# One row of the second MLP matrix in two unequal transfers, ahead of the last eleven rows

## The chip, the cores and the metric

The kernel runs on one core of a Trainium2 chip. The metric is the device time of one execution in microseconds. The core has five engines with instruction queues of their own: PE (TensorE), DVE (VectorE), ACT (ScalarE), POOL (GpSimd) and SP (SyncE, which here issues nearly all DMAs). The DMAs are carried out by 16 DMA engines.

## The reference

One decoding step for 8 sequences of one token of width 576. An attention over a cached window and an MLP work on the tokens, and a gate mixes them.

```python
g = sigmoid((x * gate_w).sum(-1, keepdims=True))
# attention: 32 query heads, 16 cached heads, the last W = 2048 positions, width 128
q = (x @ wq) -> heads
p = softmax(q k^T / sqrt(128));  a = (p v) @ wo
# MLP: 576 -> 4608 -> 576
h = gelu(layernorm(x2) @ w1 + b1);  b = h @ w2 + b2
out = g * a + (1 - g) * b
```

In the kernel both branches take the same `x` (`A_x`). The caches are 8 x 16 x 8192 x 128 values of 2 bytes each, of which the last 2048 positions are read; `w2` is 4608 x 576.

## The kernel before, in words

A planner (`_Plan`) takes operations with dependencies and costs, simulates the engines, and so fixes the order of each engine's queue; `emit` writes the queues and puts a semaphore wait ahead of an operation for every other engine or DMA that it depends on. Operations on one engine run in the order of the plan.

All bulk data goes through one chain of DMAs on SP, each issued after the one before (`after=last_dma[-1:]`): the query matrix, the first MLP matrix, then by a list named `stream` the 16 key items and 16 value items of 4 MB each, four parts of the output projection, the second bias (`bias`, L734, eight rows of 576 values), and at last the second MLP matrix (`m2_chunk`, L738 to L754). They fill four slots of a large buffer in turn; a DMA into a slot waits until its last reader is done.

The second MLP matrix stands in memory so that partition p holds its rows 36 p to 36 p + 35; a "row" below is one of these 36 rows in each of the 128 partitions, 576 values or 1152 bytes per partition. `M_CUTS` cuts the 36 rows into transfers: `[[12, 12], [8, 3, 1]]`, that is two transfers of twelve rows into one slot, then eight, three and one into the next. Each transfer has a semaphore of its own (`t0` to `t4`) and is followed by a group of matmuls on PE (`AccGroup`, written at L565): two matmuls of 288 columns a row, added up in one PSUM bank. The group waits for its transfer and runs after the group before it. After the first twelve rows four dummy matmuls (`keep_warm`, L717) keep PE going. When all groups are done, DVE and ACT copy one half each of the result (L779, L780) and SP and ACT send it out (L782).

Of the kernel before, what the change touches and what calls it, by code (L numbers as in the profile page):

```python
# [38 lines left out]
class _Plan:  # L39
# [10 lines left out]
    def add(self, eng, fn, deps=(), name=None, cost=0.1, after=(), prio=0):  # L50
        op = _Op(eng, fn, deps, name, cost, after=after, prio=prio)
        op.idx = len(self.all)
        self.all.append(op)
        return op

    def dma(self, eng, fn, semkey, nbytes, deps=(), name=None, after=(), prio=0):
        op = _Op(eng, fn, deps, name, self.DMA_ISSUE, after=after, is_dma=True, dma_sem=semkey, nbytes=nbytes, prio=prio)
        op.idx = len(self.all)
        self.all.append(op)
        return op  # L60
# [121 lines left out]
def build_kernel(nc, A_x, A_k_cache, A_v_cache, A_wq, A_wo, B_x, B_w1, B_b1, B_w2, B_b2, gate_w, out):  # L182
    B, Sq, D = A_x.shape
# [10 lines left out]
    ND = 4  # L194
# [15 lines left out]
    with ExitStack() as es:  # L210
# [77 lines left out]
        def aoffs(name):  # L288
            return R[name][0] // 2
# [4 lines left out]
        def view(name, parts=128):  # L294
            o, n, dt = R[name]
            a = arena[0:parts, o // 2: o // 2 + (n * (2 if dt == BF else 4)) // 2]
            if dt == F32:
                a = a.bitcast(F32)
            return a
# [46 lines left out]
        def slot(s):  # L346
            return RAW[:, s * DE:min((s + 1) * DE, ND * DE + SE)]
# [8 lines left out]
        def col(i, parts=128):  # L356
# [10 lines left out]
        OC = 64  # L367

        eng_sems = {e: es.enter_context(nc.semaphore("sem_" + e)) for e in ENGS}
        dma_keys = ["x", "b", "b2", "wq", "w1", "out"] + ["s%d" % i for i in range(ND + 1)] + ["t%d" % i for i in range(5)]  # L370
        dma_sems = {k: es.enter_context(nc.semaphore("dma_" + k)) for k in dma_keys}

        P = _Plan()
        add, dma = P.add, P.dma
# [7 lines left out]
                   deps=[o_idf], name="r8", cost=0.2)  # L382
# [30 lines left out]
        for s in range(2):  # L413
            o_xz.append(add("dve", (lambda s=s: lambda e: e.tensor_copy(xz[:, s, :].rearrange("p (k z) -> p k z", z=2)[:, :, s], x_sb[:, 512:576]))(),  # L414
                            deps=dx + [o_xz0], name="xz%d" % s, cost=0.12))
# [12 lines left out]
        for s in range(2):  # L428
            o_yz.append(add("dve", (lambda s=s: lambda e: e.tensor_copy(yz[:, s, :].rearrange("p (k z) -> p k z", z=2)[:, :, s], y_bf[:, 512:576]))(),
                            deps=[o_y, o_yz0], name="yz%d" % s, cost=0.12))  # L430
# [117 lines left out]
        o_hT = add("dve", lambda e: e.transpose(view("hT"), bass.AP(arena, offset=aoffs("hb"), ap=[[AST, 128], [1, FT], [FT, 32]])), deps=[o_hf], name="hT", cost=1.3)  # L548
# [25 lines left out]
        for vi in range(Hkv):  # L574
# [2 lines left out]
                stream.append(("W", vi // NVW))  # L577
            if vi + 3 < Hkv:
                stream.append(("K", vi + 3))
        M_CUTS = [[12, 12], [8, 3, 1]]  # L580
        stream += [("B", 0)] + [("M", i) for i in range(len(M_CUTS))]

        last_dma = [d_w1r]
        slot_free = [[o_qp], [], [], [o_hp], [o_qp, o_hp]]
# [12 lines left out]
        def take_slot():  # L597
            n = n_slot[0]
            n_slot[0] += 1
            return (1, 2, 0, 3)[n % ND]  # L600
# [111 lines left out]
        def keep_warm(name, n, after):  # L712
            def fn(e):
                mm = None
                for k in range(n):
                    args = (ps[:, k % 4, :], zeros_bf, maskR)
                    mm = e.matmul(*args, start=True, stop=True, skip_group_check=True) if k == 0 else held_matmul(nc, e, *args, start=True, stop=True, skip=True)  # L717
                return mm
            return add("pe", fn, deps=[exp_done[NG - 1], o_z, o_mR], name=name, cost=0.22 * n, after=after)
# [11 lines left out]
        o_m2 = []  # L731
# [6 lines left out]
        def m2_chunk(ci):  # L738
            s = take_slot()
            j = sum(sum(c) for c in M_CUTS[:ci])  # L740
            at = 0
            src = B_w2.rearrange("(p j) n -> p (j n)", j=FT)
            ops = []
            for n, jn in enumerate(M_CUTS[ci]):
                d = dma("sp", (lambda j=j, jn=jn, at=at: lambda e: e.dma_start(slot(s)[:, at * D:(at + jn) * D], src[:, j * D:(j + jn) * D]))(),
                        "t%d" % (sum(len(c) for c in M_CUTS[:ci]) + n), 128 * jn * D * 2, deps=slot_free[s] if n == 0 else [], name="d_w2_%d_%d" % (ci, n), after=last_dma[-1:])
                last_dma.append(d)
                mms = [(hT[:, j + k, 0:8], slot(s)[:, (at + k) * D:(at + k + 1) * D]) for k in range(jn)]
                ops.append(AccGroup("m2_%d_%d" % (ci, n), mms, [o_hT, d], cost=0.25 * jn, after=o_m2[-1:]).op)
                o_m2.append(ops[-1])  # L750
                if j == 0:
                    o_m2.append(keep_warm("warm1", 4, [ops[-1]]))
                j, at = j + jn, at + jn
            slot_free[s] = ops  # L754
# [15 lines left out]
        for kind, i in stream:  # L770
            {"K": k_item, "V": v_item, "W": wo_chunk, "M": m2_chunk, "B": bias}[kind](i)
# [37 lines left out]
def bass_gated_mix__sliding_block_cached__mixer_channel_mlp__decode_kernel(  # L809
    nc: bass.Bass,  # L810
    A_x: bass.AP,
    A_k_cache: bass.AP,
    A_v_cache: bass.AP,
    A_wq: bass.AP,
    A_wo: bass.AP,
    B_x: bass.AP,
    B_w1: bass.AP,
    B_b1: bass.AP,
    B_w2: bass.AP,
    B_b2: bass.AP,  # L820
    gate_w: bass.AP,
    out: bass.AP,
):
    build_kernel(nc, A_x, A_k_cache, A_v_cache, A_wq, A_wo, B_x, B_w1, B_b1, B_w2, B_b2, gate_w, out)
# [28 lines left out]
```

## Time and profile before

| | us |
|---|---|
| median of 3 runs | 366.87 (366.44 to 367.72) |
| profiled execution, its own time | 366.56 |
| its span, first to last instruction | 364.7 |
| PE busy | 242.6 |
| DVE busy | 217.3 |
| matmuls of L565 (in all 140) | 12.6 |
| issue of the five transfers of L745 | 328.01 to 334.89 |
| last copy of the result (DVE, L779) begins | 362.55 |

The span runs from the first to the last instruction that the profile records; the profiled execution's own time has some two microseconds more around it. The page gives busy time per engine, the busy share of the DMA engines in 40 slices, the chain of work that ended last, and groups of instructions by line. 154.31 MB are read from memory in the span, 423 GB/s.

### The profile page before, as it was taken

The page shows a single profiled execution, that of the slowest core. Times are in us where ns is not written, and L with a number is a line of the kernel's source. Part 1 is how long each engine was busy: PE and PEld are TensorE (multiplying, and loading weights), DVE is VectorE, ACT ScalarE, POOL GpSimd, SP SyncE. Part 2 cuts the span into 40 slices and gives each one's busy share as a digit, 9 for nine tenths or more (in the row PEclk, how much of TensorE's full clock was granted, in tenths as well). Part 3 has the DMA queues.
Part 4 walks back from the last instruction along what each step waited for, and adds up shares of the span by engine and source line. Part 5 has one row for each costly group of instructions (what it writes and reads, how often), then busy time and mean ns, then how long its engine had stood idle before and what let it go on. Part 6 is the DMA issues. An engine that isn't in the chain of part 4 may idle for free.

```text
span 364.7 us, 2619 instructions
## 1 busy us (share of the span) xinstructions
PE 242.6 (67%) x1329; PEld 57.0 (16%) x893; DVE 217.3 (60%) x160; ACT 39.9 (11%) x46; POOL 23.2 (6%) x66
## 2 busy tenths in 40 slices
PE   0346566599397956859197956868197948686675
PEld 0100000122011121202011121202011220102232
DVE  0722999666884757266774657276766668284220
ACT  1012100400400040000400040000400040002000
POOL 7210001000100100001000100001000100000000
PEclk9985599699979976969778976969798976989699
DMA  8999999999999999999999999999999999999995
GB/s 348 432 410 429 431 431 431 431 431 430 429 431 431 429 428 431 433 431 433 429 431 431 433 431 429 431 433 431 431 429 431 426 431 429 431 431 431 426 437 244
DMA packets 10675, 154.48 MB, mean 424 GB/s; under 512 B 764, under 2 KB 932, under 8 KB 1320
## 3 DMA queue, kind: packets, MB, share of 16 engines
q1 hardware_dynamic: 10608, 154.29, 99.0%
q8 instruction: 9, 0.15, 0.1%
q10 hardware_dynamic: 56, 0.03, 0.0%
q14 instruction: 2, 0.02, 0.0%
HBM read 154.31 MB, written 0.01 MB: 423 GB/s over the span
## 4 chain that ended last, share of the span: by engine, by line
DMA 58%; DVE 22%; PE 15%; issue 2%; ACT 1%; ACTq 0%; POOL 0%; DVEq 0%
DMA arena<-in_A_k_cache_dram 49%; DVE arena L649 18%; PE ps L175 9%; DMA arena<-in_B_w_dram 7%; PE ps L661 2%; DMA arena<-in_gate_w_dram 2%; PE ps L683 2%; PE ps L486 1%; DVE arena L548 1%; DVE arena L622 1%; ACT ps L631 1%; PE ps L565 0%; ACT arena L522 0%; DVE arena L543 0%; DVE arena L506 0%
## 5 line engine op out<-in xcount | busy, mean ns | idle before, releaser
L649 DVE STREAM_TRANSPOSE arena<-arena 128x2048 f32<-128x2048 f32 x64 | 144.5, 2291 | 60.0 <-DMA arena<-in_A_k_cache_dram 38.6
L175 PE MATMUL ps<-arena 128*128 128x512 bf16 (+2 forms) x453 | 136.3, 457 | 39.7 <-DVE arena L649 36.6
L683 PE MATMUL ps<-arena 128*32 128x512 bf16 x512 | 60.3, 390 | 3.1 <-DVE arena L637 2.0
L661 PE MATMUL ps<-arena 128*128 128x512 bf16 x114 | 50.5, 443 | 17.7 <-DVE arena L649 17.7
L626 ACT ACTIVATE arena<-ps,arena 128x2048 bf16<-128x2048 f32 x8 | 15.7, 1967 | 239.5 <-DVE arena L625 239.5
L661 PEld LDWEIGHTS ps<-arena 128*128 128x128 bf16 x128 | 13.9, 109 | 171.0 <-DVE arena L649 113.5
L683 PEld LDWEIGHTS ps<-arena 128*32 128x32 bf16 x512 | 25.1, 99 | 46.6 <-issue 20.4
L622 DVE TENSOR_REDUCE arena<-ps 128x1 f32<-128x2048 f32 x8 | 18.3, 2286 | 12.5 <-PE ps L175 12.4
L616 POOL COPY arena<-arena 32x128 bf16<-32x128 bf16 x32 | 9.2, 287 | 212.7 <-PE ps L175 202.9
L633 DVE STREAM_TRANSPOSE arena<-arena 128x2048 bf16<-128x2048 bf16 x8 | 18.3, 2291 | 6.4 <-ACT arena L626 6.4
L693 DVE SCALAR_TENSOR_TENSOR arena<-ps,arena 128x512 f32<-128x512 f32 x8 | 6.0, 752 | 20.2 <-PE ps L683 20.2
L565 PE MATMUL ps<-arena 128*8 128x288 bf16 (+1 forms) x140 | 12.6, 339 | 7.1 <-DVE arena L708 5.8
L702 PE MATMUL ps<-arena 128*128 128x256 f32 x16 | 5.6, 431 | 16.0 <-POOL arena L698 16.0
L635 PE MATMUL ps<-arena 128*128 128x1 f32 x16 | 4.5, 353 | 15.1 <-ACT ps L631 14.3
L631 ACT ACTIVATE ps<-arena 128x2048 f32<-128x2048 f32 x7 | 13.1, 1875 | 0.1
L698 POOL TENSOR_TENSOR arena<-arena 128x256 f32<-128x256 f32 x8 | 4.9, 612 | 109.4 <-DVE arena L625 61.7
L440 PE MATMUL ps<-arena 8*128 8x8 bf16 x8 | 0.6, 171 | 14.7 <-DVE arena L414 9.6
L696 DVE TENSOR_REDUCE arena<-arena 128x128 f32<-128x512 f32 x8 | 8.4, 1047 | 0.3
L565 PEld LDWEIGHTS ps<-arena 128*8 128x8 bf16 (+1 forms) x140 | 6.4, 97 | 13.5 <-DVE arena L708 7.0
L705 ACT ACTIVATE arena<-ps,arena 64x256 bf16<-64x256 f32 x8 | 3.7, 464 | 42.9 <-PE ps L702 42.8
L708 DVE STREAM_TRANSPOSE arena<-arena 128x256 bf16<-128x256 bf16 x4 | 2.5, 632 | 9.8 <-ACT arena L705 9.8
L543 DVE TENSOR_TENSOR arena<-arena 128x1152 f32<-128x1152 f32 x1 | 1.4, 1359 | 11.3 <-ACT arena L541 11.3
(86 smaller groups left out, 64.5 us busy)
## 6 DMA issues: line engine op xcount, KB each, us to landing
arena<-in_A_k_cache_dram SPq DMA_DIRECT2D x16, 4096.0 KB, 28.0
arena<-in_A_v_cache_dram SPq DMA_DIRECT2D x16, 4096.0 KB, 32.6
arena<-in_B_w_dram SPq DMA_DIRECT2D x1, 4608.0 KB, 23.4
arena<-in_A_wo_dram SPq DMA_DIRECT2D x4, 1152.0 KB, 34.1
arena<-in_A_wq_dram SPq DMA_DIRECT2D x1, 4096.0 KB, 12.9
arena<-in_B_w_dram SPq DMA_DIRECT2D x2, 1728.0 KB, 27.7
arena<-in_B_w_dram SPq DMA_DIRECT2D x1, 1152.0 KB, 27.1
arena<-in_B_w_dram SPq DMA_DIRECT2D x1, 576.0 KB, 24.3
```

What stands on the lines that cost most here:

```text
L175: return e.add_instruction(mybir.InstMatmult(name=nc.get_next_instruction_name(), engine=mybir.EngineType.PE, ins=[e.lower_ap(rhs), e.lowe ...
L565: ins = e.matmul(ps[32 * j:32 * j + 8, BK_ACC, 0:JN], lhsT, rhs[:, JN * j:JN * j + JN], start=False, stop=True, skip_group_check=True, til ...
L616: return e.tensor_copy(dst, src)
L622: mx = add("dve", lambda e: e.tensor_reduce(out=k(MX), in_=ps[:, 0:4, :].rearrange("p a n -> p (a n)"), axis=AXL.X, op=ALU.max), deps=[qk_ ...
L626: ex = add("act", lambda e: e.activation(out=Pm, in_=ps[:, 0:4, :].rearrange("p a n -> p (a n)"), func=ACTF.Exp, bias=k(NB), scale=SCALE, ...
L631: mask_done[g + 1] = add("act", lambda e: e.activation(out=ps[:, 0:4, :].rearrange("p a (n c) -> p (a n) c", c=4), in_=bass.AP(arena_f, of ...
L633: pt_done[g] = add("dve", lambda e: e.transpose(bass.AP(arena, offset=aoffs("PT") + 2048 * (g % 2), ap=[[AST, 128], [8, 64], [512, 4], [1, ...
L649: tr = add("dve", (lambda h=h, kb=kb: lambda e: e.transpose(bass.AP(arena_f, offset=foffs("KT") + kb * 2048, ap=[[AST // 2, 128], [1, 2048]]),
L661: mm = e.matmul(*args, start=False, stop=True, skip_group_check=True) if rc == 0 else held_matmul(nc, e, *args, stop=True, skip=True)
L683: mm = e.matmul(ps[c:c + 32, BK_OS[g % 2], :], PT[:, g % 2, 16 * c + 32 * t:16 * c + 32 * t + 32], slot(s)[:, (j % 2) * SE + 512 * t:(j % ...
L693: vmul = add("dve", lambda e: e.scalar_tensor_tensor(out=vmv, in0=ps[:, BK_OS[g % 2], :].rearrange("p (r d) -> p r d", r=4), scalar=rr[:, ...
L696: acc_ev[g] = add("dve", lambda e: e.tensor_reduce(out=EV[:, g % 2, :], in_=vm.rearrange("p (r d) -> p d r", r=4), axis=AXL.X, op=ALU.add) ...
```

## The change

The last twelve rows are cut `[1, 7, 3, 1]` in place of `[8, 3, 1]`. The first of these four, one row, is fetched by two transfers: partitions 0 to 113 with semaphore `t6`, then partitions 114 to 127 with semaphore `t5`. As the change's description has it, the first uses six DMA engines (19 partitions each) and the second fourteen (one partition each). The row's group of two matmuls waits for both. The other rows follow as before in whole transfers, with semaphores `t2` to `t4`. SP thus issues seven transfers of the second matrix and not five.

```diff
-        dma_keys = [...] + ["t%d" % i for i in range(5)]
+        dma_keys = [...] + ["t%d" % i for i in range(7)]
...
-        M_CUTS = [[12, 12], [8, 3, 1]]
+        NSK = 114
+        M_CUTS = [[12, 12], [1, 7, 3, 1]]
...
             for n, jn in enumerate(M_CUTS[ci]):
-                d = dma("sp", (lambda j=j, jn=jn, at=at: lambda e: e.dma_start(slot(s)[:, at * D:(at + jn) * D], src[:, j * D:(j + jn) * D]))(),
-                        "t%d" % (sum(len(c) for c in M_CUTS[:ci]) + n), 128 * jn * D * 2, deps=slot_free[s] if n == 0 else [], name="d_w2_%d_%d" % (ci, n), after=last_dma[-1:])
-                last_dma.append(d)
+                parts = ((0, NSK, 6), (NSK, 128, 5)) if (ci, n) == (1, 0) else ((0, 128, 2 * ci + n - (ci > 0)),)
+                ds = []
+                for p0, p1, key in parts:
+                    d = dma("sp", (lambda j=j, jn=jn, at=at, p0=p0, p1=p1: lambda e: e.dma_start(slot(s)[p0:p1, at * D:(at + jn) * D], src[p0:p1, j * D:(j + jn) * D]))(),
+                            "t%d" % key, (p1 - p0) * jn * D * 2, deps=slot_free[s] if n == 0 else [], name="d_w2_%d_%d_%d" % (ci, n, p0), after=last_dma[-1:])
+                    last_dma.append(d)
+                    ds.append(d)
                 mms = [(hT[:, j + k, 0:8], slot(s)[:, (at + k) * D:(at + k + 1) * D]) for k in range(jn)]
-                ops.append(AccGroup("m2_%d_%d" % (ci, n), mms, [o_hT, d], cost=0.25 * jn, after=o_m2[-1:]).op)
+                ops.append(AccGroup("m2_%d_%d" % (ci, n), mms, [o_hT] + ds, cost=0.25 * jn, after=o_m2[-1:]).op)
```

More of the change, by code (lines that the diff above doesn't have):

```diff
@@ L369, in build_kernel @@
         eng_sems = {e: es.enter_context(nc.semaphore("sem_" + e)) for e in ENGS}
-        dma_keys = ["x", "b", "b2", "wq", "w1", "out"] + ["s%d" % i for i in range(ND + 1)] + ["t%d" % i for i in range(5)]
+        dma_keys = ["x", "b", "b2", "wq", "w1", "out"] + ["s%d" % i for i in range(ND + 1)] + ["t%d" % i for i in range(7)]
         dma_sems = {k: es.enter_context(nc.semaphore("dma_" + k)) for k in dma_keys}
```

## The prediction

> **What bounds the kernel now.** I read the page first, then the chain of waits, the timeline of the end, the issues of line 745, and busy time by stage.
>
> ```profile
> span 364.7 us, 2619 instructions
> DMA  8999999999999999999999999999999999999995
> q1 hardware_dynamic: 10608, 154.29, 99.0%
> q8 instruction: 9, 0.15, 0.1%
> ```
>
> The DMA engines are full from the second slice to the last, so the kernel lasts as long as its bytes, and an edit at the end of the stream counts only through the moment at which the last bytes are used. The chain of waits from 355 us says which moment that is:
>
> ```profile
> 333.61 27.14 DMA arena<-in_B_w_dram
> 360.75 0.04 issue
> 360.79 1.74 PE ps L565 x24
> 362.53 0.02 issue
> 362.55 0.45 DVE arena L779
> ```
>
> The end hangs on the landing of the eight-row transfer at 360.75 us. Its 16 matmuls, the 6 of the three-row and the 2 of the one-row transfer run without a pause (24 in 1.72 us, so 72 ns each); the rest, 362.53 to 364.73, is eviction and output. The timeline of PE and of SP:
>
> ```profile
> 357.98 1.64 PE L565 MATMUL ps<-arena 128*8 128x288 bf16 x24
> 360.79 1.72 PE L565 MATMUL ps<-arena 128*8 128x288 bf16 x24 [1.17 <-DMA arena<-in_B_w_dram]
> ...
> 328.01 6.88 SPq L745 DMA_DIRECT2D arena<-in_B_w_dram  x5
> ```
>
> PE is idle for 1.17 us before 360.79, and SP has issued all five second-matrix transfers by 334.9, over 24 us before the last part lands. Busy time by stage of the last two microseconds (last two columns: mean busy share of the 16 DMA engines, GB/s):
>
> ```profile
> 360.60:361.00 0.40, 0.21 (x4) 0.18 (x6) 0.00 (x0) 0.00 (x0) 0.00 (x0) 1.00 0.60 242
> 361.00:361.40 0.40, 0.40 (x10) 0.27 (x8) 0.00 (x0) 0.00 (x0) 0.00 (x0) 1.00 0.47 182
> 361.40:361.70 0.30, 0.30 (x10) 0.18 (x4) 0.00 (x0) 0.00 (x0) 0.00 (x0) 1.00 0.46 161
> 361.70:362.00 0.30, 0.30 (x8) 0.12 (x6) 0.00 (x0) 0.00 (x0) 0.00 (x0) 1.00 0.07 23
> ```
>
> 0.47 x 16 is 7.5: half of the engines are out of work by 361 us, the other half run to 361.8. A transfer lands when its slowest engine is done, so moving bytes from the late half to the early half would bring the end forward. All depends on which half the six engines belong to.
>
> **Which engines are late, and why.** The trace has a record of every DMA packet (queue, start, duration, bytes) without the engine's number. On one engine a packet starts 3 to 4 ns before the last one's end, so the packets can be strung into 16 chains. The bias transfer has 8 rows; eight chains carry its 1152-byte packets (347.6 to 349.2 us). The gate transfer of 6 rows marks six chains at 4.75 to 4.93 us, and following these to the end (the order of the chains' lags stays the same but for the jumps told below) leads to six of those eight. The last packet of each engine starts at (us):
>
> ```
> six engines with gate rows   360.31 360.34 360.58 360.74 361.10 361.64
> two more with bias rows      360.09 361.55
> the other eight              360.53 360.54 361.63 361.68 361.76 361.77 361.79 361.85
> ```
>
> The reason for the two halves is the queue of instructions: nine 16 KB packets (q8, above) at 32, 90, 129, 174, 220, 267, 306, 344 and 362 us. Each of the first eight puts one chain 1.41 to 1.43 us behind, for the rest of the run, since its queue never runs empty; two 8 KB fetches (83 and 180 us) cost 0.84 and 0.52 us. The fetch at 344 us hit one of the six.
>
> **The change part by part.** Durations are pitches of packets in the same records: 1152 bytes 47 ns, 3456 bytes 132, 9216 bytes 344, a transfer's end mark 6. That is 36.8 ps a byte and 4.4 ns a packet, so 8064 bytes (seven rows) cost 301.
>
> *Rows moved.* Before, each engine carries 8 x 344 + 6 = 2756 ns of the eight-row transfer. After, all carry 8 x 301.4 + 6 = 2417 for seven rows. 114 rows on six engines are 19 each: 19 x 47 + 6 = 897; 14 on fourteen are one each: 47 + 6 = 53. So the six go to 3367 (+0.61 us), eight others to 2470 (-0.29), and the two left out to 2417 (-0.34). The small-packet pitch is bounded by 42 ns (bytes alone: +0.51 in all) and 60 ns, the slowest of the undisturbed 1152-byte packets at the start (+0.88); 47 is taken, as it was measured in this stage.
>
> *The end, with these shifts.* Of the six, the latest ends at 361.64 + 0.61 = 362.25; of the others the latest moves from 361.85 to 361.56. The last packet is thus 0.40 us later than before. Packets' starts and landings lie 0.3 us apart here (361.85 and 362.13, the last of the 16 updates). With that lag seven rows land at 361.11, three at 362.17, one at 362.55. PE does 14 matmuls from 361.15 to 362.15, six from 362.21 to 362.64, two to 362.78. The same sum for before gives 362.47 (the profile: 362.53), so the change costs **+0.31 us**: less than 0.40 because the first row's two matmuls leave the tail.
>
> *That first row.* Its two landings come at about 358.7 (12 rows of the late one of the six done at 357.4, then 0.95 us, then the lag), PE is busy with the twelve rows before until 359.62, so the added wait for a second semaphore ends in the 1.17 us gap. Queued behind it on PE is only the rest of the second matrix. Without that cover it costs its two matmuls, 0.14 us.
>
> *Two more issues on SP.* Line 745's issues take 328 to 434 ns: 0.87 us more, done by 335.8, past nothing but the output issue at 363.02. Free; the cover is 22 us.
>
> *Two more transfers.* In a queue that is never empty nothing of a transfer's fixed price shows: the one-row transfer's last landing follows that of the three rows by 0.32 us (361.81 and 362.13 in the updates), and its bytes need 8 x 47 = 0.38. So two more are counted at nothing beyond their end marks. [...]
>
> **The sum.** Span 364.73 + 0.31 = 365.04; the profiled execution took 366.56, so 1.83 lie around the span: 366.87. That execution is 0.31 below the median of the three runs (366.87), on which the forecast stands: 366.87 + 0.31 = **367.2 us**. 0.3% is 1.1 us, about what a measurement of this kernel can tell from no change, so that counts as no change.
>
> **Rivals.**
> *All six are early (0.21).* If the fetches fall on other engines in other executions, and none of the 16 KB ones on the six, the latest of the six is the one at 361.10 + 0.61 = 361.71, the others end at 361.56; the seven rows land at 360.57 and PE ends at 362.24 (by the others alone at 362.09): -0.23 to -0.38 us, 366.5 to 366.6. For it: a single fetch, the one at 344 us, is all that stands against it here. Against: eight fetches on 16 engines would by chance nearly always hit one of six.
> *A fetch in the tail (0.06).* The ninth 16 KB fetch starts at 362.02, after the last data packet. The change has an engine of the six work until 362.25. If the fetch comes on a loaded one of the six, it adds its 1.42 us to the 0.31: 368.6, slower. It decides from the point where the fetch starts before that engine's last packets. Against: one engine in 16, and PE's progress, which it follows, is itself 0.3 us later.
> *Fixed time that shows (0.03).* At the start, with an empty queue, the 512 KB transfer lands 3.6 us after its issue (the issues' list), 1.2 of them for its bytes (32 KB an engine at 36.8 ps). If each of the two added transfers drained the queue for the other 2.4 us, the time would be 366.87 + 4.8 + 0.31 = 372.0. [...] Against: no gap stands between any two of the last transfers.
> *No shift (0.04).* If the 114 rows went eight to an engine as in whole transfers, there would be no skew; only 47 + 12 ns more, 366.9. For: no transfer of the trace has more than 16 rows and a count that 16 does not divide. Against: the six-row transfer ends on six updates.
> *Forecast (0.66).* Its own range is 366.8 to 367.8: the packet bounds (+0.22 and +0.57), and the runs' scatter (366.44 to 367.72).
>
> The whole range goes from 366.3, under the gain, to 367.9; outside lie the fetch, the fixed time and the far ends of the scatter. Faster by over 0.3% would need 1.1 us, and even a perfect levelling of the 16 ends above (mean 361.12, last 361.85) is worth 0.73: 0.04, for scatter. Slower: 0.13 (0.09 of the two rivals, 0.04 scatter). Same: 0.83.
>
> **What the changed profile would show.** Two matmuls of line 565 near 359.6, then 14, 6 and 2 from about 361.15, with short waits for DMA between them; the DMA share near 0.38 (six of 16) or less after 361.6 where it was 0.46; the last landing at 362.5; more packets of 1152 bytes (128 more). SP shows seven issues ending by 336. The forecast is wrong if the late engine is not of the six (last landing below 362.0), if the bias and gate chains were misread, or if the second part's transfer opens a gap between packets.

## The result, and the profile after

The change makes the kernel slower: 367.89 us, median of 9 runs (367.60 to 369.17), against 366.66 us for the kernel before (9 runs, 366.37 to 367.72). The ratio is 1.0036 (95% interval 1.0021 to 1.0051), so about 1.2 us where 0.3 was forecast. The forecast time was 367.2. The profiled execution took 367.60 us with a span of 365.8, so again 1.8 lie around the span; against the profiled execution of before it is 1.04 us longer.

The page of after, the lines that answer to those of before:

```profile
span 365.8 us, 2640 instructions
DMA  8999999999999999999999999999999999999995
q1 hardware_dynamic: 10756, 154.29, 98.9%
q8 instruction: 8, 0.13, 0.1%
```

The bytes of queue q1 are the same, in 148 more packets, and in tenths the DMA row is digit for digit that of before. Nothing on this page shows what happened.

The chain of waits of after, from 334 us on (start, length, what):

```profile
334.36 27.43 DMA arena<-in_B_w_dram
361.79 0.04 issue
361.83 1.02 PE ps L565 x14
362.86 0.04 issue
362.89 0.68 PE ps L565 x8
363.57 0.02 issue
363.59 0.45 DVE arena L784
```

On this chain the end still hangs on the first big transfer of the tail, now seven rows, which lands at 361.79. Fourteen matmuls follow at 73 ns, then PE waits for the three rows and does the last eight. Of these the last two start at 363.26, just behind the landing of the last row at 363.22, so that landing sets the end as well. All matmuls are done at 363.57, where the prediction had 362.78 and before had 362.53.

The timeline of PE (the bracket gives the idle time ahead and what ended it), of the weight loads (PEld) of its last two matmuls, and of SP's issues:

```profile
358.49 1.76 PE L565 MATMUL ps<-arena 128*8 128x288 bf16 x26 [0.63 <-DMA arena<-in_B_w_dram]
361.83 1.72 PE L565 MATMUL ps<-arena 128*8 128x288 bf16 x22 [1.58 <-DMA arena<-in_B_w_dram]
...
363.26 0.09 PEld L565 LDWEIGHTS ps<-arena 128*8 128x8 bf16 x2
...
328.06 15.69 SPq L749 DMA_DIRECT2D arena<-in_B_w_dram  x7
```

The first row's two matmuls have left the tail: 26 and 22 in place of 24 and 24. But the group before the tail is late too: it begins at 358.49, after a wait of 0.63 us for a DMA, where before it began at 357.98 without one. The second twelve rows, which the change does not touch, landed half a microsecond late (358.45 against 357.94), while the first twelve rows were still on time (353.85 against 353.84). So the loss begins ahead of the tail.

Busy time by stage shows where. The columns are window, length, busy shares of PE, PEld, DVE, ACT and POOL, TensorE clock, mean share of the DMA engines, and GB/s. First before, then after:

```profile
357.00:358.00 1.00, 0.83 (x5) 0.02 (x4) 0.00 (x0) 0.00 (x0) 0.00 (x0) 1.00 0.98 415
358.00:359.00 1.00, 1.00 (x18) 0.74 (x20) 0.00 (x0) 0.00 (x0) 0.00 (x0) 1.00 1.00 423
359.00:360.00 1.00, 0.62 (x11) 0.23 (x6) 0.00 (x0) 0.00 (x0) 0.00 (x0) 1.00 0.97 402
```

```profile
357.00:358.00 1.00, 0.87 (x4) 0.00 (x0) 0.00 (x0) 0.00 (x0) 0.00 (x0) 1.00 0.87 258
358.00:359.00 1.00, 0.51 (x10) 0.38 (x12) 0.00 (x0) 0.00 (x0) 0.00 (x0) 1.00 1.07 331
359.00:360.00 1.00, 1.00 (x22) 0.70 (x16) 0.00 (x0) 0.00 (x0) 0.00 (x0) 1.00 0.98 397
...
361.40:361.70 0.30, 0.00 (x0) 0.00 (x0) 0.00 (x0) 0.00 (x0) 0.00 (x0) 1.00 0.74 284
361.70:362.00 0.30, 0.17 (x4) 0.14 (x6) 0.00 (x0) 0.00 (x0) 0.00 (x0) 1.00 0.60 215
362.00:362.40 0.40, 0.40 (x10) 0.30 (x8) 0.00 (x0) 0.00 (x0) 0.00 (x0) 1.00 0.13 46
```

In the two microseconds from 357 on, when the packets of the split row are moved, the DMA engines are as busy as ever (0.87 and 1.07, where a packet is counted whole in one window) but move 258 and 331 GB/s in place of 415 and 423. The engines are occupied and slow. The records of single packets say it without the windows' edges:

```
packets that start from 355 to 362.5 us, after   shortest ns longest ns  (before: all alike)
13824 bytes (second twelve rows)                    516        691         516
 8064 bytes (seven rows)                            305        491     9216 bytes: 347
 1152 bytes (split row, last row)                    51         82          51
rate by 0.4 us from 357.0: 339 310 299 294 328 361 417 GB/s   (before: 430 427 429 429 428 424 424)
```

The first longer packet starts at 356.3 us. From 357.25 to 359.25 every data packet that starts, of whatever size, is longer than its like before, by 1.06 to 1.6 times, and by 1.5 on average at the worst; no packet takes as long as a microsecond there, so all 16 engines are hit. From 359.5 on all data packets are within 7% of their old length. Called the *excess* below: the time of all packets above their undisturbed time, over 16 engines. Here it is 0.61 us an engine.

### The profile page after: what moved, and what is told of

Its sections match the earlier page's. It is cut to its first block, busy times and chain, and to the rows that moved or that the text cites. A ratio compares the mean times of both kernels' runs of the same rounds, so it can differ in the third digit from the quotient of the medians.

```text
span 365.8 us, 2640 instructions
## 1 busy us (share of the span) xinstructions
PE 247.7 (68%) x1347; PEld 57.6 (16%) x893; DVE 217.1 (59%) x160; ACT 39.9 (11%) x46; POOL 23.2 (6%) x66
## 4 chain that ended last, share of the span: by engine, by line
DMA 58%; DVE 24%; PE 14%; issue 1%; ACT 1%; ACTq 0%; POOL 0%; SPq 0%; DVEq 0%
DMA arena<-in_A_k_cache_dram 49%; DVE arena L650 20%; DMA arena<-in_B_w_dram 7%; PE ps L175 7%; PE ps L662 2%; DMA arena<-in_gate_w_dram 2%; PE ps L684 2%; PE ps L486 1%; DVE arena L548 1%; DVE arena L623 1%; ACT ps L632 1%; PE ps L565 0%; ACT arena L522 0%; DVE arena L543 0%; DVE arena L506 0%
## 5 line engine op out<-in xcount | busy, mean ns | idle before, releaser
L662 PE MATMUL ps<-arena 128*128 128x512 bf16 x128 | 57.5, 450 | 51.3 <-DVE arena L650 51.2
```

Source lines behind the costliest of these rows:

```text
L662: mm = e.matmul(*args, start=False, stop=True, skip_group_check=True) if rc == 0 else held_matmul(nc, e, *args, stop=True, skip=True)
```

## The experiments

After this comparison two theories stood: the cost is the uneven load of the six engines alone, as forecast (and only its size was off), or the split transfer slows the whole stream while it is moved. For the second it was open what makes it: the count of partitions, the reads, small packets, or the place where the packets are written. Excess and longest packets below are worked out from the packet records of one profiled execution each; times are medians, and ratios are against the kernel before on the same chip.

**The change without the split.** `whole_row` keeps the cut `[1, 7, 3, 1]` and fetches the first row in one transfer of 128 partitions:

```diff
-                parts = ((0, NSK, 6), (NSK, 128, 5)) if (ci, n) == (1, 0) else ...
+                parts = ((0, 128, 6),) if (ci, n) == (1, 0) else ...
```

> Cuts 1, 7, 3, 1 as in the changed kernel, but the first row in one transfer of 128 partitions. In the profile of the change all packets between 357.0 and 359.4 us are stretched, 8064-byte ones from 305 to as much as 491 ns. Theory A (the six engines write into partitions that other engines are serving, and this slows all of them): no stretch here, 8064-byte packets at 305 ns; 0.1 to 0.2 us under the kernel before, since the first row's two matmuls leave the tail (-0.14). Theory B (the cut into one and seven rows slows the packets): the stretch stays, 0.4 to 0.8 us above the kernel before. Theory C (only uneven load counts, the stretch comes with it): as A here.

366.73 us, ratio 0.9998 (0.9986 to 1.0011). Busy time by stage:

```profile
357.00:358.00 1.00, 0.84 (x5) 0.10 (x1) 0.00 (x0) 0.00 (x0) 0.00 (x0) 1.00 0.98 395
358.00:359.00 1.00, 0.88 (x15) 0.60 (x16) 0.00 (x0) 0.00 (x0) 0.00 (x0) 1.00 0.98 412
```

No dip, all 128 packets of 8064 bytes at 305 ns. The new cut by itself is worth nothing that these runs can tell; the cost is that of the split. The 0.14 us expected of it do not show: PE ends at 362.74, 0.35 behind the landing of the last row (362.39), and that landing does not come earlier for the new cut (362.13 in before).

**The split with even load.** `split_112_16` has `NSK = 112`: 112 partitions, then 16. In the traces of before and after, transfers of 6, 8, 14, 114 and 128 partitions land with 6, 8, 14, 6 and 16 updates, each the largest number up to 16 that divides the partitions; by that count both parts here go over all 16 engines.

> The changed kernel with the first row split 112 + 16 partitions: by the count that divides, both parts go over sixteen engines, seven and one partitions each, so the load is even as before, but most engines write a few partitions that belong to the share of another engine in whole transfers. Theory A: a smaller stretch, some 0.1 to 0.4 us above the whole row. Theory C: no stretch, within 0.05 us of the whole row (one more packet and end mark per engine).

367.48 us, ratio 1.0011 (0.9999 to 1.0023). By that count every engine has the same load here, and yet packets are stretched (8064 bytes up to 486 ns, excess 0.38) and the rate dips:

```profile
357.00:358.00 1.00, 0.84 (x5) 0.06 (x1) 0.00 (x0) 0.00 (x0) 0.00 (x0) 1.00 1.01 348
358.00:359.00 1.00, 0.38 (x9) 0.28 (x10) 0.00 (x0) 0.00 (x0) 0.00 (x0) 1.00 1.06 353
```

So the stretch is not a matter of load. Against the kernel before, its time is within the measurement of no change; the packets show the stretch, and the spans of its twelve runs (365.1 to 365.8) lie at or above those of `whole_row` (364.6 to 365.1).

**Extra transfers.** The other runs but the last take the kernel *before* and issue one extra transfer ahead of the eight rows, into columns of the slot that nothing reads, with a semaphore that only the final wait looks at. The outputs do not depend on it. The frame is the same in all, and only the destination, source and byte count differ (`pad_from_chip` also depends on its constant):

```diff
+            if ci == 1:
+                pad = dma("sp", lambda e: e.dma_start(DESTINATION, SOURCE), "t5", ...,
+                          deps=slot_free[s], name="d_pad", after=last_dma[-1:])
+                last_dma.append(pad)
+                pads.append(pad)
...
-        add("sp", lambda e: e.sem_inc(eng_sems["sp"], 1), deps=fin, name="final_wait", cost=0.05)
+        add("sp", lambda e: e.sem_inc(eng_sems["sp"], 1), deps=fin + pads, name="final_wait", cost=0.05)
```

`pad_six_own` was meant to load six engines without mixing their partitions, `pad_six_spread` is shaped as the change's first part (102 partitions, 17 to an engine):

```diff
+ slot(s)[0:48:8, 12 * D:28 * D]     # pad_six_own, 16 pieces of 1152 bytes in each of 6 partitions
+ slot(s)[0:102, 12 * D:13 * D]      # pad_six_spread, src[0:102, 24 * D:25 * D]
```

> The kernel before (cuts 8, 3, 1), with one extra transfer ahead of the eight rows that nothing reads: partitions 0, 8, 16, 24, 32 and 40, sixteen pieces of 1152 bytes each, so six engines get 16 packets more (16 x 47 + 6 = 0.76 us) and each is meant to write a partition of its own share. Theory A: no stretch; the late one of the six ends 0.76 later, 0.55 past the latest before, so about +0.45 to +0.55 us. Theory C: stretch as in the change, +0.9 to +1.2 us.

> The kernel before with one extra transfer ahead of the eight rows that nothing reads: 102 partitions of 1152 bytes, 17 to each of six engines (17 x 47 + 6 = 0.81 us), written over partitions 0 to 101, that is mostly outside the share of the engine that writes. Theory A: the stretch comes back, +1.0 to +1.4 us. Theory C: the same as the six in their own shares plus 0.05.

368.26 us, 1.0034 (1.0021 to 1.0047), excess 0.61; and 367.72 us, 1.0027 (1.0017 to 1.0038), excess 0.55. Both stretch the stream (9216 bytes up to 716 and 596 ns). `pad_six_own` did not do what it was meant for: six partitions in steps of eight do not leave the stream alone. Six in steps of four do, in `pad_six_home` further down (347 ns).

Then count, reads and the source's place. 120 partitions from either end; 102 partitions from a constant in on-chip memory (`ones_bf`, 1024 bytes each), so that large memory is not read; and 102 partitions from one row of large memory (`B_b2`):

```diff
+ slot(s)[0:120, 12 * D:13 * D]          # pad_120_low
+ slot(s)[8:128, 12 * D:13 * D]          # pad_120_high
+ slot(s)[0:102, 12 * D:12 * D + 512]    # pad_from_chip, source ones_bf[0:102, :]
+ slot(s)[0:102, 12 * D:13 * D]          # pad_one_row, source B_b2.partition_broadcast(102)
```

> The kernel before with an extra transfer ahead of the eight rows that nothing reads: partitions 0 to 119, 1152 bytes each; 120 goes over fifteen engines, eight partitions each, so every engine stays in the share that it has in a transfer of 128. Theory A (writing outside the own share slows everything): packets of the eight rows stay at 347 ns; +0.3 to +0.4 us for the eight packets. Theory D (many short reads from scattered rows of memory by fewer engines slow everything): little or no stretch, since fifteen of sixteen read as in a whole transfer. Theory E (any transfer that is not spread over sixteen engines slows what follows): stretch, +0.9 us or more.

> The same with partitions 8 to 127: fifteen engines, eight partitions each, each engine now in the share of the next one. Theory A: stretch, the eight-row packets well over 347 ns, +0.8 us or more. Theory D: as partitions 0 to 119. Theory E: stretch in both.

> The kernel before with an extra transfer of 102 partitions, 1024 bytes each, copied from a constant tile in on-chip memory to the unused part of the slot: six engines, 17 partitions each, no read of the large memory. Theory A: stretch as with 102 partitions from memory (packets of the eight rows to 1.3 times 347 ns). Theory D: no stretch.

> The kernel before with an extra transfer of 102 partitions of 1152 bytes that all read the same 1152 bytes of memory (the second bias), written as in the spread pad: six engines, 17 partitions each. Theory A: stretch as with the 102 scattered rows. Theory D: no stretch, unless reading one row over and over is slow by itself.

All four stretch the stream (table below). `pad_120_low` was to leave it alone if a whole transfer gives every engine eight neighbouring partitions; it does not (540 ns for 347), so either the shares are not of that kind or theory A is wrong. The copy from on-chip memory does it with up to 467 ns for 347, so no read of large memory is needed, and by `pad_one_row` (491 ns) no scattered one. The nearest suspect left is the writing side. The next four vary the partitions written, with one load: 8 packets of 1152 bytes on each of 16 engines.

```diff
+ slot(s)[:, 12 * D:13 * D]            # pad_128, one piece in each of 128 partitions
+ slot(s)[0:128:8, 12 * D:20 * D]      # pad_16_every_8th, 8 pieces in each of 16
+ slot(s)[0:16, 12 * D:20 * D]         # pad_16_first, 8 pieces in each of 16
+ slot(s)[0:64, 12 * D:14 * D]         # pad_64, 2 pieces in each of 64
```

> Control: the kernel before with an extra transfer of all 128 partitions, 1152 bytes each, ahead of the eight rows, read by nothing. Theory F (a transfer slows all engines while its writes are under way when its engines write other partitions than in a whole transfer) and theory G (every transfer of fewer than 128 partitions does): no stretch, packets of the eight rows at 347 ns; +0.38 us for eight packets on each engine.

> The same 128 packets of 1152 bytes, eight to an engine, but as 16 partitions (0, 8, 16 to 120) with eight pieces each: sixteen engines, engine e meant to write partition 8e, which is its own if a whole transfer gives each engine eight neighbouring partitions. Theory F with such shares: no stretch. Theory G, and F with shares that interleave: stretch, packets of the eight rows over 400 ns.

> The same with partitions 0 to 15, eight pieces each: engine e meant to write partition e. Theory F with neighbouring shares: strong stretch, since all sixteen engines write what two of them own. F with interleaved shares (partition p to engine p modulo 16): no stretch. Theory G: stretch.

> The same with partitions 0 to 63, two pieces each, so sixteen engines with four partitions each. Theory F with neighbouring shares: stretch (only engine 0 and a few others stay at home). With interleaved shares: none. Theory G: stretch. If only counts that are no power of two do it: none.

The control costs its own bytes (8 x 47 = 0.38 us by the prediction's pitch; 0.42 by the medians) and stretches nothing. The other three carry the same bytes on as many engines and cost more, the most where only 16 neighbouring partitions are written. Now the place alone: 16 pieces in each of 8 partitions, 4 apart, so that eight engines carry 16 packets each in both kernels. Only the first partition differs, 0 or 64 (the rows read from large memory move along with it). *Home* and *away* are names for these two sets; that the first would leave the stream alone and the second not was the author's assumption:

```diff
+ slot(s)[0:32:4, 12 * D:28 * D]      # pad_8_home
+ slot(s)[64:96:4, 12 * D:28 * D]     # pad_8_away
+ slot(s)[0:24:4, 12 * D:28 * D]      # pad_six_home: the first six of these partitions
```

> The kernel before with an extra transfer that nothing reads: eight partitions 0, 4, 8 to 28, sixteen pieces of 1152 bytes each, ahead of the eight rows. [...] Theory G (every transfer of fewer than 128 partitions slows all engines): stretch, +1.2 us or more, as with six engines.

> [...] Theory G: the same as with partitions 0 to 28.

> Only six engines at home: partitions 0, 4 to 20, sixteen pieces each. [...] Theory G: stretch, +1.2 us as with six engines at partitions 0, 8 to 40.

Busy time by stage of `pad_8_home`, then of `pad_8_away`:

```profile
357.00:358.00 1.00, 0.81 (x3) 0.00 (x0) 0.00 (x0) 0.00 (x0) 0.00 (x0) 1.00 0.96 393
358.00:359.00 1.00, 0.97 (x16) 0.72 (x18) 0.00 (x0) 0.00 (x0) 0.00 (x0) 1.00 1.05 445
359.00:360.00 1.00, 0.66 (x12) 0.27 (x6) 0.00 (x0) 0.00 (x0) 0.00 (x0) 1.00 1.01 423
```

```profile
357.00:358.00 1.00, 0.84 (x9) 0.10 (x1) 0.00 (x0) 0.00 (x0) 0.00 (x0) 1.00 0.92 227
358.00:359.00 1.00, 0.29 (x2) 0.00 (x0) 0.00 (x0) 0.00 (x0) 0.00 (x0) 1.00 0.98 247
359.00:360.00 1.00, 0.20 (x4) 0.17 (x6) 0.00 (x0) 0.00 (x0) 0.00 (x0) 1.00 1.04 258
```

The same packets on as many engines, written to other partitions: 393 to 445 GB/s in one, 227 to 258 in the other for three microseconds, at the same busy share. At home all 128 packets of 9216 bytes take 347 ns, which rules out theory G; away they take up to 702. All the extra transfers:

```
                    load      packets     excess   longest of 9216 bytes   us       ratio (95% interval)
                    us/engine on engines  us/eng.  (alone: 347 ns)
pad_128             0.38      16          0        347                     367.06   1.0017 (1.0008-1.0027)
pad_64              0.38      16          0.77     649                     368.47   1.0048 (1.0031-1.0064)
pad_16_every_8th    0.38      16          0.72     655                     368.13   1.0042 (1.0027-1.0057)
pad_16_first        0.38      16          1.32     1026                    368.57   1.0053 (1.0038-1.0068)
pad_120_low         0.38      15          0.36     540                     367.69   1.0019 (1.0008-1.0031)
pad_120_high        0.38      15          0.38     531                     367.65   1.0020 (1.0010-1.0031)
pad_six_spread      0.80       6          0.55     596                     367.72   1.0027 (1.0017-1.0038)
pad_from_chip       -          6          0.33     467                     367.82   1.0020 (1.0008-1.0032)
pad_one_row         0.80       6          0.50     491                     368.17   1.0032 (1.0020-1.0044)
pad_six_own         0.76       6          0.61     716                     368.26   1.0034 (1.0021-1.0047)
pad_six_home        0.76       6          0        347                     367.34   1.0019 (1.0009-1.0030)
pad_8_home          0.76       8          0        347                     367.28   1.0010 (0.9999-1.0021)
pad_8_away          0.76       8          1.42     702                     368.96   1.0055 (1.0041-1.0070)
```

Load is packets times the pitch of 47 ns; for the copy from on-chip memory no pitch is given, since its packets were measured only amid the stretch. Where load and engines agree, the difference in time is about the difference in excess: away minus home 1.68 us by the medians for 1.42, `pad_16_first` minus `pad_128` 1.51 for 1.32, `pad_six_own` minus `pad_six_home` (two chips) 0.92 for 0.61. `pad_six_home` is the uneven load of the change's kind with nothing stretched. Its chain of waits:

```profile
335.01 26.82 DMA arena<-in_B_w_dram
361.83 0.04 issue
361.87 1.75 PE ps L565 x24
363.62 0.02 issue
363.64 0.45 DVE arena L785
```

The eight rows land 1.08 us later than in the profile of before, but this execution was behind already ahead of the extra transfer: its first twelve rows landed at 354.35, 0.51 later than before's. That leaves 0.57 us as the price of the load.

**A finer tail.** Since the end hangs on a transfer's landing plus its matmuls, `cuts_1_6_3_1_1` cuts the last rows finer, all transfers whole:

```diff
-        M_CUTS = [[12, 12], [8, 3, 1]]
+        M_CUTS = [[12, 12], [1, 6, 3, 1, 1]]
```

> A version meant to be faster: whole transfers only, the last twelve rows cut 1, 6, 3, 1, 1 and not 8, 3, 1. The last landing stays where it is (two more end marks), but PE then has only two matmuls left after it: the end 0.1 to 0.2 us earlier than before, 0.05 to 0.15 under the whole row with 1, 7, 3, 1. If the chain of landings alone counts, no change.

366.74 us, ratio 1.0000 (0.9991 to 1.0008). The chain of waits now ends with one row's two matmuls:

```profile
336.60 25.87 DMA arena<-in_B_w_dram
362.47 0.04 issue
362.52 0.31 PE ps L565 x2
362.83 0.03 issue
362.85 0.45 DVE arena L779
```

The last row lands at 362.47 here, where it was expected to stay at before's 362.13, and the last copy starts at 362.85 against 362.55. Of these 0.34 and 0.30 us, 0.21 were there before the tail began (first twelve rows at 354.05). Two matmuls that start on a landing take 0.31 us, not 2 x 72 ns, so PE ends about 0.35 us behind the last landing. Before ended 0.40 behind it (362.13 and 362.53), so hardly anything was there to be gained: the bytes' own end is the bound.

## Why the prediction was wrong

**The step that failed** is in the change part by part: "Durations are pitches of packets in the same records", and below it, of the small packets, "47 is taken, as it was measured in this stage". In the undisturbed stream those pitches are exact (51 ns as a duration, 47 or 48 as a pitch, in `pad_8_home` on all 256 packets), and the mistake was to carry them over to a stream with the split row in it. That the split row would slow the *other* transfers was nowhere among the costs. The bounds of 42 and 60 ns were for the row's own packets; the larger part of the loss is on the packets of 13824 and 8064 bytes around it. The term that is missing is 0.61 us an engine. The trace of before gave no warning of it: the only such transfer in its full stream, the bias of 8 rows, is eight packets of 1152 bytes spread over 1.6 us, and none of those nor of the packets of 13824 bytes beside them is stretched (51 and 516 ns). One small packet at a time, then, does not do it.

How that comes out at the end: the last packet starts at 362.74 against 362.25 forecast (+0.49), and from there to the landing of the last row (363.22) it is 0.48 us where 0.30 was forecast (+0.18), together +0.67. The seven rows land at 361.79 against 361.11 (+0.68), the three at 362.85 against 362.17 (+0.68). The +0.18 belongs to the disturbed runs too: from the last packet's start to the last landing it is 0.28 to 0.37 us in the runs without stretch and 0.40 to 0.48 in those with it, and why is open. The last eight matmuls take 0.68 us where 6 and 2 at 72 ns make 0.57, which gives the rest of the 0.79 by which PE ends late. That is a second, smaller term mis-sized: the sum let the last two matmuls end 0.23 us behind the last landing (362.55 and 362.78), and they end 0.35 behind it (363.22 and 363.57), as in `whole_row` and `cuts_1_6_3_1_1`.

**The cause, as far as it is shown.** Whether the stream slows depends on which partitions the extra transfer writes, with as many engines, packets and bytes: packets of 9216 bytes take 347 ns in `pad_8_home` and up to 702 in `pad_8_away`. The rows that these two read differ as well; no run holds them fixed, and that the place of the reads is not it rests on `pad_from_chip` and `pad_one_row`, which stretch (467 and 491 ns) without scattered reads of large memory. With eight packets an engine, the excess is 1.32 us an engine for 16 neighbouring partitions, 0.77 for 64, 0.72 for every eighth, 0.36 and 0.38 for 120, and 0 for all 128. The number of partitions is not all that counts: 16 of them cost 1.32 or 0.72, and eight of them, with 16 packets from each of eight engines, 1.42 or nothing.

Why the place counts is not shown. The records of packets name neither the engine nor the partition, so which partitions an engine writes in a whole transfer can't be read from them, and whether packets wait for each other where they are written can't either: the runs show what the stretch depends on, not a queue. They do show that one transfer of 128 partitions is better than two over parts of them (0.9998 whole, 1.0036 split). Why the whole stream slows is open too: in `pad_six_own` ten engines carry no extra packet, and still every packet that starts from 357.6 to 358.5 is 1.35 to 2.1 times as long as alone.

**The uneven load** was of the right sign and about the right size. The prediction's steps, applied to `pad_six_home` (0.76 us more on the six, the latest of them from 361.64 to 362.40, so 0.55 past 361.85, and no row taken out of the tail), give +0.55; 0.64 was measured by the medians (366.70 and 367.34; the interval of the ratio allows 0.3 to 1.1), and 0.57 by the profile less what it was behind. For the change that leaves the +0.31 standing beside the stretch: 0.31 + 0.68 for the landings + 0.11 for the matmuls = 1.10, and PE in fact ends 1.04 later than before (363.57 and 362.53). The sum is 0.06 over since the prediction reckoned before's own end 0.06 too early (362.47).

**Which engines are late.** In after the six landings of the row's first part come at 357.60, 57.85, 58.05, 58.34, 58.81 and 59.37 us: one of the six is again late, as read from the bias and gate chains, and the rival in which all six are early did not happen. It could not have been told from the median.

**The covers.** The first row's matmuls are hidden, as forecast: its last part lands at 359.59 and PE is busy with the twelve rows until 360.1. SP's seven issues were forecast to end by 336; they end at 343.75, since the last two took 4.72 and 4.21 us:

```profile
L749 SPq DMA_DIRECT2D arena<-in_B_w_dram x7: 287/374/4717, 328.1 to 339.5; - x7
```

(shortest, median and longest in ns). With 18 us left to the landing this cost nothing. Nor did the two transfers show a fixed time: no gap opened, and that rival is out. A fetch in the tail did not come either: after has eight fetches on q8 in the span where before had nine; the ninth starts at 366.8, past the span's end. That fetches follow PE's progress holds only roughly: between one 16 KB fetch and the next PE starts 231 to 282 recorded instructions in before and 232 to 266 in after up to the eighth, but the ninth of after comes 3.2 us behind PE's last matmul. The rival "no shift" is out by the six landings of the row's first part.

**The signs named beforehand.** The matmul groups (two hidden, 14, then 6 and 2) came as forecast but late by 0.5 to 0.8 us. The DMA share of 0.38 or less "after 361.6" came out at 0.74 and 0.60 up to 362.0 and 0.13 after it: with the whole stream late by over half a microsecond, more engines were still at work. The last landing was to be at 362.5 and came at 363.2. The list of what would make the forecast wrong had the late engine, the chains and gaps between packets on it, and not packets that grow longer while the queue stays full.

## What to carry to other kernels

In a stream that keeps all DMA engines full, use transfers over all 128 partitions (`pad_128`: no packet stretched). Of the smaller ones, two stretched nothing: eight partitions 0, 4 to 28 and six partitions 0, 4 to 20 (347 ns). Every other transfer of 100 to 150 KB that was tried here slowed the whole stream while it was moved, by 0.3 to 1.4 us; the bias of eight packets did not (51 and 516 ns). A high DMA share says that the engines are occupied, not that they move bytes (1.04 at 258 GB/s in `pad_8_away`, 1.05 at 445 in `pad_8_home`): read the GB/s column beside it, and the length of equal packets. To level late engines, a small transfer would have to be uneven in engines and written where nothing is stretched (here partitions 0, 4 to 20), and it would be worth at most what lies between the mean and the last of the engines' ends, 0.73 us here. No run tried one that takes load off the late engines.

## What the runs showed of the hardware

- A transfer of 16 neighbouring partitions, 147 KB in packets of 1152 bytes, stretches packets of 9216 bytes in the transfer behind it from 347 to as much as 1026 ns (`pad_16_first`).
- The stretch needs no read from large memory: a copy within on-chip memory does it (`pad_from_chip`: 467 ns for 347).
- A fetch of 16 KB of instructions puts one DMA engine 1.41 to 1.43 us behind for the rest of the run (before). In after the last of the six engines was again behind the other five (359.37 against 357.60 to 358.81).
- Two issues on SP took 4.72 and 4.21 us where their neighbours took 0.3 to 0.4, with nothing on the page to explain it. In five other profiles the last issue took 3.0 to 4.8 us, and `split_112_16`, with seven issues as well, has none.
- Two matmuls of 288 columns that start on a landing take 0.31 us (`cuts_1_6_3_1_1`); in a run of 24 without a pause they take 0.14 (before).
